# Retention attention with float32 scores in every unit, one bank pair a unit, and a prologue in a fixed order

## The chip, the cores and the metric

One core of one Trainium2 chip. The metric is device time in microseconds (us) of one execution; the kernel before takes 932.51 us in the median of three runs (931.04 to 933.9).

## What is computed

Three stages in a row, all float32: a linear attention with a decay for each head, and two feed-forward layers with unusual activations.

```python
# q, k, v: (4, 8, 768, 64); gamma per head
state = gamma * state + k_t (outer) v_t;  y_t = scale * q_t @ state      # for t in 768
x = y as 3072 tokens x 512
h = x @ w_in (512 x 2048);   g = h if h >= 1, 0 if h <= -1, else (h + 1)**2 / 4
x2 = g @ w_out (2048 x 512)
h = x2 @ w2_in (512 x 1024); solu = h * softmax(h); out = layernorm(solu) * g_ln @ w2_out
```

The weights of both layers arrive as float64.

## The kernel before

**Attention in units.** The recurrence is done in chunks of 128 tokens, six chunks a batch and four batches: 24 units. A unit (`attention`, L131) has *scores* (keys times queries, decayed by the table `dmat`, giving `sm`) and *products*: `pv` takes the state of the units before (L206, with `qn`, the decayed queries) and `sm` times values (L210); `sp` (L216) is the unit's own contribution to the state. `split` (L88) cuts `pv` into a rounded part `xh` and a remainder `xl`. Heads go in pairs; a head has 64 rows, so o = 0 and o = 1 are the two halves of the array. Units 0 to 7 multiply scores in float32 (L163). Units 8 to 23 load every half twice, make a rounded key with its remainder stacked below it and a rounded query with its remainder beside it, and multiply those (L188, 256 columns), add two result halves (L191, L192) and apply the table (L193).

**Tokens in blocks, features in slots.** Four units make a block of 512 tokens, six blocks in all. A slot is one block against one piece of 128 features: `moe_h` (L299), 12 products into `hp` (L306), then the activation (L312 to L314) and its split into `gh`, `gl`; two slots later `moe_out` (L320), 12 products into four accumulators `acc` (L334). All 12 have 512 columns in the rounded float32 format. The slots run in segments: block 0 with features 0 to 5, block 1 with 0 to 11, block 0 with 6 to 15, block 1 with 12 to 15, then blocks 2 to 5 whole. Blocks 0 and 1 therefore write a part of their sum to DRAM (`x2p`) and load it again at the end of their second segment (L346), through the ring of three `cs` buffers that the activation uses too.

**Weights.** `load_w` (L96) brings a float64 piece of 512 KB, `conv_w` (L101) makes a rounded part and a remainder from it on VectorE and ScalarE, five VectorE instructions a piece, two pieces a feature. This happens in the slots of the first four segments.

**What sets the order.** The Tile framework orders the instructions by its own timing model. The queue SP issues every DMA in program order, and each engine runs its own queue in order. Scores and products of a unit take buffers of one bank each (`ps_acc` in block 0, then `ps_a`).

**The last stage** (L402 on) goes by tiles of 128 tokens: `h2p`, softmax and norm statistics, transposes `tp`, products `op`. The change touches in it only how `h2` gets two of its banks.

Of the kernel before, what the change touches and what calls it, by code (L numbers as in the profile page):

```python
# [9 lines left out]
F32 = mybir.dt.float32  # L10
# [12 lines left out]
C = 128  # L23
# [12 lines left out]
NF32 = 2 * CPB  # L36
GATE = 2 * CPB
STEP0 = 7
W0 = -4
WARM = 40  # L40
PER = 4
# [8 lines left out]
def kernel(  # L50
# [16 lines left out]
    ve, sc, gp, pe = nc.vector, nc.scalar, nc.gpsimd, nc.tensor  # L67
# [7 lines left out]
    ps_a = ctx.enter_context(tc.tile_pool(name="ps_a", bufs=2, space=bass.MemoryType.PSUM))  # L75
# [18 lines left out]
    state = {}  # L94

    def load_w(src, pool=wp):  # L96
        raw = pool.tile([128, 512, 2], U32, tag="w", name="w_raw")
        state["last_w"] = nc.sync.dma_start(raw.rearrange("p a t -> p (a t)"), src.bitcast(U32))
        return raw

    def conv_w(raw, scale=None):  # L101
# [10 lines left out]
        ve.scalar_tensor_tensor(mu, hw, 0x80000000, mu, op0=ALU.bitwise_and, op1=ALU.bitwise_xor)  # L112
        ve.tensor_tensor(out=mi, in0=mi, in1=p.bitcast(I32), op=ALU.add)  # L113
        w = wp.tile([128, 2, 512], F32R, tag="w", name="w")
        hi, lo = w[:, 0, :], w[:, 1, :]
        if scale is None:
            sc.activation(hi, m, AF.Copy)
            ve.tensor_tensor(out=lo, in0=m, in1=fl(hi), op=ALU.subtract)
# [3 lines left out]
        return hi, lo  # L122


# [6 lines left out]
    def attention(u, env):  # L131
# [4 lines left out]
        ppool, ptag = (ps_acc, "acc") if blk == 0 else (ps_a, "pa")  # L136
        exact = u < NF32
        kv = (wp if exact else attp).tile([128, 2, H, D], F32, tag="w" if exact else "kv", name="kv",
                                          bufs=None if exact else 1)
        qn = None  # L140
        with (ExitStack() if u < GATE else tc.issue_after(state["last_w"].ins)):
            if exact:
                qk = wp.tile([128, 2, NPAIR, C], F32, tag="w", name="qk")
                nc.sync.dma_start(qk, qk_t[b, c])
            else:
                qks = []
                for o in range(2):
                    qk = attp.tile([128, 2, NPAIR, C], F32, tag="qk", name="qk", bufs=2)
                    for dup in range(2):
                        nc.sync.dma_start(qk[64 * dup:64 * dup + 64], qk_t[b, c, 64 * o:64 * o + 64])  # L150
                    qks.append(qk)
                if not first:
                    qn = attp.tile([128, NPAIR, C], F32, tag="qn", name="qn", bufs=1)
                    nc.sync.dma_start(qn, qk_t[b, c, :, 0])
            nc.sync.dma_start(kv, kv_t[b, c])
        yield
        if exact:
            yield
            qp = [ppool.tile([128, NPAIR, C], F32, tag=ptag, name=f"qp{o}") for o in range(2)]
            for p in range(NPAIR):  # L160
                for o in range(2):
                    r = slice(64 * o, 64 * o + 64)
                    pe.matmul(qp[o][:, p, :], qk[r, 1, p, :], qk[r, 0, p, :], start=True, stop=True)  # L163
            if not first:
                qn = attp.tile([128, NPAIR, C], F32, tag="qn", name="qn", bufs=1)
                ve.tensor_tensor(out=qn, in0=qk[:, 0], in1=qdec, op=ALU.mult)
        elif not first:
            gp.tensor_tensor(out=qn, in0=qn, in1=qdec, op=ALU.mult)
        if not last:
            gp.tensor_tensor(out=kv[:, 0], in0=kv[:, 0], in1=vdec.to_broadcast([128, H, D]), op=ALU.mult)  # L170
        sm = []
        for o in range(2):
            t = attp.tile([128, NPAIR, C], F32, tag="sm", name="sm", bufs=2)
            if exact:
                ve.tensor_tensor(out=t, in0=qp[o], in1=dmat[:, o], op=ALU.mult)
            else:
                raw = qks[o]
                kh = cv.tile([128, NPAIR, C], F32R, tag="wm", name="kh", bufs=3)
# [5 lines left out]
                yield  # L184
                for g in range(2):
                    qpo = ppool.tile([128, 2, 2, C], F32, tag=ptag, name=f"qp{g}")
                    for p in range(2):
                        pe.matmul(qpo[:, p].rearrange("a b c -> a (b c)"), kh[:, 2 * g + p, :],  # L188
                                  qs[:, 2 * g + p].rearrange("a b c -> a (b c)"), start=True, stop=True)
# [5 lines left out]
            if not exact and o == 0:  # L195
                yield
# [22 lines left out]
        if last:  # L219
            return  # L220
# [346 lines left out]
```

## Time and profile before

| | |
|---|---|
| median of 3 runs | 932.51 us |
| profiled execution | 931.13 us, span 929.3 us |
| TensorE (PE) busy | 909.6 us, 98% |
| VectorE (DVE) | 700.1 us, 75% |
| ScalarE (ACT) | 395.8 us, 43% |
| GpSimd (POOL) | 48.3 us, 5% |
| granted TensorE clock, mean | 0.995 |
| DMA | 87.16 MB, mean 94 GB/s |

Busy time is a union of intervals whose ends are modelled, so 98% does not say that PE runs at its rate. To see where it does, count instructions: a stretch of the span holds so many products, each product has a shortest spacing in steady work, and what is left of the stretch was lost. The span has four parts: the prologue to the first `hp` product, the slots of blocks 0 and 1 with the weight conversion, the slots of blocks 2 to 5 with the remaining attention, and from about 644 us on the last stage.

### The profile page before, as it was taken

What the parts mean: (1) busy time and instruction counts of PE and PEld (TensorE: products, weight loads), DVE (VectorE), ACT (ScalarE), POOL (GpSimd) and SP (SyncE); (2) the same over time, 40 slices, a digit from 0 to 9 for tenths busy, and PEclk for the clock granted to TensorE, in tenths of its full rate; (3) what the DMA queues carried; (4) which work ended last, traced back from release to release, by engine and by line L of the source; (5) the groups of instructions that cost most, each with busy time, mean ns of one, the idle gap of its engine ahead of it and who ended that gap; (6) DMA issues with size and microseconds to landing.
All of it is one profiled execution on the core that took longest, in us unless ns stands there. A gap on an engine that the chain in (4) does not pass through costs nothing.

```text
span 929.3 us, 12929 instructions
## 1 busy us (share of the span) xinstructions
PE 909.6 (98%) x4808; PEld 754.5 (81%) x4808; DVE 700.1 (75%) x1542; ACT 395.8 (43%) x757; POOL 48.3 (5%) x42
## 2 busy tenths in 40 slices
PE   8898999999889999999999999999999999999998
PEld 7686888888768888888888888888888888888886
DVE  5999999846675666676576549953988888888884
ACT  3656766533444444444444327632333333333322
POOL 3200101000101110011100000000000000000000
PEclk9999999999999999999999999999999999999999
DMA  9930752205553323332234104121101010100000
GB/s 342 417 137 1 238 159 75 84 1 153 153 170 94 100 81 98 96 93 78 69 103 152 53 1 160 45 94 46 45 35 68 24 68 24 68 24 23 24 23 35
DMA packets 29839, 87.16 MB, mean 94 GB/s; under 512 B 4176, under 2 KB 4304, under 8 KB 29008
## 3 DMA queue, kind: packets, MB, share of 16 engines
q1 hardware_dynamic: 29776, 86.34, 28.5%
q8 instruction: 38, 0.62, 0.3%
q14 instruction: 25, 0.20, 0.1%
HBM read 71.64 MB, written 14.68 MB: 93 GB/s over the span
## 4 chain that ended last, share of the span: by engine, by line
PE 91%; DVE 5%; DMA 2%; issue 1%; ACT 0%; SPq 0%; POOL 0%; ACTq 0%; DVEq 0%; POOLq 0%
PE acc L334 27%; PE hp L306 27%; PE h2p L433 14%; PE op L485 14%; PE tp L474 2%; PE pv L210 2%; PE pv L206 2%; PE qp L188 1%; DMA qk<-in_qk_t_dram 1%; PE sp L216 1%; PE qp L163 1%; DVE wm L112 1%; DVE wm L113 1%; DMA xs<-x2p 1%; DMA vdec<-in_vdec_dram 0%
## 5 line engine op out<-in xcount | busy, mean ns | idle before, releaser
L306 PE MATMUL hp<-xh,w 128*128 128x512 f32 x768 | 200.1, 395 | 7.2 <-DVE cs L314 2.9
L334 PE MATMUL acc<-gh,w 128*128 128x512 f32 x768 | 198.4, 391 | 1.6 <-DVE xs L347 1.6
L306 PEld LDWEIGHTS hp<-xh,w 128*128 128x128 f32 x768 | 141.9, 189 | 38.5 <-DVE cs L314 3.7
L334 PEld LDWEIGHTS acc<-gh,w 128*128 128x128 f32 x768 | 143.1, 188 | 32.3 <-DVE xs L347 2.3
L313 ACT ACTIVATE cs<-cs,half 128x512 f32<-128x512 f32 x96 | 69.3, 723 | 138.9 <-DVE cs L312 138.5
L334 PE MATMUL acc<-gl,w 128*128 128x512 f32 x384 | 110.7, 391 | 0.0
L306 PE MATMUL hp<-xl,w 128*128 128x512 f32 x384 | 105.7, 392 | 0.1
L433 PE MATMUL h2p<-w,x2h 128*128 128x512 f32 x384 | 97.0, 395 | 0.0
L312 DVE TENSOR_SCALAR cs<-hp 128x512 f32<-128x512 f32 x96 | 65.8, 688 | 39.1 <-PE hp L306 36.0
L90 DVE TENSOR_TENSOR gl<-cs,gh 128x512 fp32r<-128x512 f32 x96 | 68.4, 713 | 33.0 <-ACT gh L89 32.5
L314 DVE TENSOR_TENSOR cs<-hp,cs 128x512 f32<-128x512 f32 x96 | 66.1, 690 | 35.3 <-ACT cs L313 35.1
L485 PE MATMUL op<-w,lh 128*128 128x512 f32 x384 | 91.3, 390 | 0.2 <-ACT lh L89 0.2
L89 ACT ACTIVATE gh<-cs 128x512 fp32r<-128x512 f32 x96 | 60.4, 629 | 58.4 <-DVE cs L314 58.2
L306 PEld LDWEIGHTS hp<-xl,w 128*128 128x128 f32 x384 | 72.0, 189 | 15.6 <-DVE xl L90 0.5
L485 PEld LDWEIGHTS op<-w,lh 128*128 128x128 f32 x384 | 71.9, 188 | 15.3 <-ACT lh L89 0.5
L334 PEld LDWEIGHTS acc<-gl,w 128*128 128x128 f32 x384 | 71.6, 188 | 15.1
L433 PEld LDWEIGHTS h2p<-w,x2h 128*128 128x128 f32 x384 | 70.5, 188 | 13.7
L443 ACT ACTIVATE e<-h2p,st 128x512 f32<-128x512 f32 x48 | 32.6, 685 | 50.1 <-DVE st L460 38.3
L182 DVE TENSOR_TENSOR kh<-qk,kh 64x512 fp32r<-64x512 f32 x32 | 25.4, 793 | 36.8 <-ACT kh L180 36.5
L433 PE MATMUL h2p<-w,x2l 128*128 128x512 f32 x192 | 51.6, 390 | 0.0
L89 ACT ACTIVATE x2h<-x2r 128x512 fp32r<-128x512 f32 x24 | 15.1, 631 | 76.8 <-PE h2p L433 59.5
L485 PE MATMUL op<-w,ll 128*128 128x512 f32 x192 | 47.7, 390 | 0.0
(76 smaller groups left out, 1169.4 us busy)
## 6 DMA issues: line engine op xcount, KB each, us to landing
qk<-in_qk_t_dram SPq DMA_DIRECT2D x64, 256.0 KB, 3.9
kv<-in_kv_t_dram SPq DMA_DIRECT2D x24, 512.0 KB, 4.6
w_raw<-in_w_in_dram SPq DMA_DIRECT2D x24, 512.0 KB, 8.4
w_raw<-in_w_out_dram SPq DMA_DIRECT2D x24, 512.0 KB, 5.8
x2d<-xs SPq DMA_DIRECT2D x24, 256.0 KB, 3.2
x2r<-x2d SPq DMA_DIRECT2D x6, 1024.0 KB, 4.8
out_dram<-o SPq DMA_DIRECT2D x24, 256.0 KB, 2.0
qk<-in_qk_t_dram SPq DMA_DIRECT2D x8, 512.0 KB, 8.7
```

The costliest lines, as they stand in the source:

```text
L89: sc.activation(hi, src, AF.Copy)
L90: ve.tensor_tensor(out=lo, in0=src, in1=fl(hi), op=ALU.subtract)
L182: ve.tensor_tensor(out=kh[64:128], in0=raw[64:128, 1], in1=fl(kh[64:128]), op=ALU.subtract)
L206: pe.matmul(pv[:, p, :], st[:, p, :], qn[:, p, :], start=(p == 0), stop=False, skip_group_check=True)
L306: pe.matmul(hp, l[:, k * 128:(k + 1) * 128], r[:, k, :], start=(n == 0), stop=(n == 3 * KD - 1))
L312: ve.tensor_scalar(cs, hp, -1.0, 1.0, op0=ALU.max, op1=ALU.min)
L313: sc.activation(cs, cs, AF.Square, bias=half, scale=0.5)
L314: ve.tensor_tensor(out=cs, in0=hp, in1=cs, op=ALU.max)
L334: pe.matmul(acc[d][:, :BLK], l[:, d * 128:(d + 1) * 128], r, start=(first and m == 1), stop=(last and m == 3))
L433: pe.matmul(hps[n], l[:, k, :], w2i[k, n][part], start=(m == 0), stop=(m == 3 * KD - 1))
L443: sc.activation(e[:, n, :], hps[n], AF.Exp, bias=st[:, 2:3], accum_out=st[:, 3 + n:4 + n])
L485: pe.matmul(op, l[:, f, :], w2o[f][part], start=(n == 0), stop=(n == 3 * NF2 - 1))
```

## The change

What it does, part by part:

- **Scores.** All 24 units take the float32 path. The rounded copies, the doubled loads, the two additions and the separate load of `qn` go. A unit has one pair of banks (`bank`): its scores, then its products `pv` in the first and `sp` in the second. Units of block 0 other than unit 2 take the pair from `ps_acc`, all others take the single buffer of `ps_a`, which is now one buffer of two banks. From unit 8 on `sm` is one VectorE instruction of 1024 elements.
- **Tables.** `dmat` and `qdec` are no longer loaded as 128 rows. One row of 1024 numbers (`xrow`) is loaded by the ScalarE queue and spread over the partitions by products with a row of ones; VectorE multiplies the result by `vdec` or `gdec`.
- **Prologue.** Block 0 and the conversion of the first weight piece are written out in a fixed order, scores a unit ahead of the products. `issue` chains the instructions of each engine so that the scheduler keeps that order. Loads of the first weights stand between the loads of block 0. The warming products go from 40 to 18.
- **Later units.** Steps are given out as load, scores and products, six or seven, two and no slots ahead; two buffers each for keys/queries and keys/values.
- **Activation.** `(relu((h+1)/2))**2`, clipped at 1 and joined with h: two ScalarE instructions and one of VectorE, where there were two of VectorE and one of ScalarE.
- **Reload.** `xs` comes back through the ScalarE queue; the stores stay on SP.

```diff
-    ps_a = ctx.enter_context(tc.tile_pool(name="ps_a", bufs=2, space=bass.MemoryType.PSUM))
+    ps_a = ctx.enter_context(tc.tile_pool(name="ps_a", bufs=1, space=bass.MemoryType.PSUM))
...
+    @contextmanager
+    def issue(fixed, engines=None):
+        done = {i.name for i in nc.cur_bb.bb.instructions}
+        yield
+        for i in nc.cur_bb.bb.instructions:
+            if i.name in done or (engines and i.engine not in engines):
+                continue
+            if i.engine in tail:
+                tc.add_manual_dep(i, tail[i.engine].name, mybir.DependencyInfo(
+                    mybir.DependencyClass.NoSync, mybir.DependencyReason.DATA), reason="order of issue")
+            if fixed:
+                tail[i.engine] = i
...
+        if blk == 0 and u != 2:
+            pa = None
+            bank = [ps_acc.tile([128, 512], F32, tag="acc", name=f"pa{o}") for o in range(2)]
+        else:
+            pa = ps_a.tile([128, 2, 512], F32, tag="pa", name="pa")
+            bank = [pa[:, o] for o in range(2)]
+        qp = [t.rearrange("a (p c) -> a p c", p=NPAIR) for t in bank]
+        for p in range(NPAIR):
+            for o in range(2):
+                r = slice(64 * o, 64 * o + 64)
+                pe.matmul(qp[o][:, p, :], qk[r, 1, p, :], qk[r, 0, p, :], start=True, stop=True)
...
-                qs = attp.tile([128, NPAIR, 2, C], F32R, tag="qs", name="qs", bufs=1)
-                sc.activation(kh, raw[:, 1], AF.Copy)
-                sc.activation(qs[:, :, 0, :], raw[:, 0], AF.Copy)
-                ve.tensor_tensor(out=kh[64:128], in0=raw[64:128, 1], in1=fl(kh[64:128]), op=ALU.subtract)
-                ve.tensor_tensor(out=qs[:, :, 1, :], in0=raw[:, 0], in1=fl(qs[:, :, 0, :]), op=ALU.subtract)
-                        pe.matmul(qpo[:, p].rearrange("a b c -> a (b c)"), kh[:, 2 * g + p, :],
-                                  qs[:, 2 * g + p].rearrange("a b c -> a (b c)"), start=True, stop=True)
...
+    def make_dmat():
+        t = ps_a.tile([128, 2, 512], F32, tag="pa", name="tab")
+        for o in range(2):
+            pe.matmul(t[:, o], ones, xrow[:, o].rearrange("a p c -> a (p c)"), start=True, stop=True)
+            ve.tensor_tensor(out=dmat[:, o], in0=t[:, o].rearrange("a (p c) -> a p c", p=NPAIR),
+                             in1=vdec[:, o::2].to_broadcast([128, NPAIR, C]), op=ALU.mult)
+            gp.affine_select(out=dmat[:, o], in_=dmat[:, o], pattern=[[0, NPAIR], [1, C]], compare_op=ALU.is_ge,
+                             fill=0.0, base=0, channel_multiplier=-1)
...
-        ve.tensor_scalar(cs, hp, -1.0, 1.0, op0=ALU.max, op1=ALU.min)
-        sc.activation(cs, cs, AF.Square, bias=half, scale=0.5)
-        ve.tensor_tensor(out=cs, in0=hp, in1=cs, op=ALU.max)
+        sc.activation(cs, hp, AF.Relu, bias=half, scale=0.5)
+        sc.activation(cs, cs, AF.Square)
+        ve.scalar_tensor_tensor(cs, cs, 1.0, hp, op0=ALU.min, op1=ALU.max)
...
-                    nc.sync.dma_start(xs, x2p[blk][:, d, :])
+                    sc.dma_start(xs, x2p[blk][:, d, :])
...
+    with issue(True):
+        sc.dma_start(xrow, xtab_d.rearrange("(a o d) p c -> d a o p c", a=1, o=2)[0])
+        sc.dma_start(gdec, gdec_d)
+        sy.dma_start(vdec, vdec_d)
+        ve.memset(ones, 1.0)
+        att(0, 2)
+        att(1, 2)
+        att(2, 2)
+        att(3, 1)
+        load_wi(0)
+        att(3, 1)
+        load_wi(1)
+        load_wo(0)
+        load_wo(1)
+        make_dmat()
...
+        cv0 = conv_steps(wraw[0][0], wi, 0)
```

**The products of units 1 and 2 on PE.** Before, the scores of unit 2 stand in two groups, one for each half of the array (`qp_295`, `qp_296`), between the products of unit 1:

```order
L206 MATMUL pv<-qn,state 128x128 x4
L216 MATMUL sp<-kv 64x64 x8
L210 MATMUL pv<-sm,kv 64x128
L163 MATMUL qp_295<-qk 128x128 x4
L210 MATMUL pv<-sm,kv 64x128 x7
L163 MATMUL qp_296<-qk 128x128 x4
```

In the change the spread of `qdec`, the products of unit 0, the scores of unit 2 (both halves in turn, one buffer `pa`) and the products of unit 1 follow in this order:

```order
L256 MATMUL tab<-xrow,ones 64x512 x2
L209 MATMUL pa_159<-sm,kv 64x128 x8
L214 MATMUL pa_160<-kv 64x64 x8
L182 MATMUL pa<-qk 128x128 x8
L205 MATMUL pa_169<-qn,state 128x128 x4
L209 MATMUL pa_169<-sm,kv 64x128 x8
L214 MATMUL pa_170<-kv 64x64 x8
```

The two halves of a unit's scores, which stood apart, now alternate, and they stand ahead of the products of the unit before.

**The end of block 1's last segment on PE**, where units 11 and 12 meet the first slots of block 2. Before (`qp_2210` and `qp_2215` are the last scores of unit 11, `qp_2371`, `qp_2376` and `qp_2422` the first of unit 12):

```order
L188 MATMUL qp_2210<-qs,kh 128x256 x2
L188 MATMUL qp_2215<-qs,kh 128x256 x2
L206 MATMUL pv<-qn,state 128x128 x4
L210 MATMUL pv<-sm,kv 64x128
L188 MATMUL qp_2371<-qs,kh 128x256 x2
L210 MATMUL pv<-sm,kv 64x128 x7
L306 MATMUL hp<-xh,w 128x512 x5
L188 MATMUL qp_2376<-qs,kh 128x256 x2
L306 MATMUL hp<-xh,w 128x512 x11
L306 MATMUL hp<-xl,w 128x512 x8
L188 MATMUL qp_2422<-qs,kh 128x256 x2
```

In the change, behind the last `acc` of block 1:

```order
L182 MATMUL pa<-qk 128x128 x8
L205 MATMUL pa<-qn,state 128x128 x4
L209 MATMUL pa<-sm,kv 64x128 x8
L324 MATMUL hp<-xh,w 128x512 x16
L182 MATMUL pa<-qk 128x128 x8
L324 MATMUL hp<-xl,w 128x512 x8
L209 MATMUL pa<-sm,kv 64x128 x8
L214 MATMUL pa<-kv 64x64 x8
```

Unit 11's scores and products stand in one piece, and unit 12's scores come once, between the first two slots of block 2; no group waits for a second load of the same keys.

## Rows read from the trace of the kernel before

**Rows 1.** Busy time of each engine in three stretches (us, engine busy and count, clock).

```profile
28.00:98.00 70.00, 64.72 (x392) 50.88 (x392) 68.43 (x130) 42.69 (x76) 3.87 (x2) 0.98 0.41 163
98.00:229.00 131.00, 131.00 (x642) 108.45 (x642) 108.03 (x186) 71.46 (x128) 8.70 (x6) 1.00 0.39 115
229.00:283.00 54.00, 48.66 (x310) 39.08 (x309) 37.55 (x65) 23.64 (x50) 6.67 (x5) 1.00 0.59 169
```

**Rows 2.** Chain that ended last, in order of time: start, us, what; steady work.

```profile
278.15 0.89 PE pv L206 x8
279.04 1.02 PE pv L210 x16
280.06 0.47 PE sp L216 x16
...
286.01 0.47 PE qp L188 x4
...
503.30 2.72 PE acc L334 x12
```

**Rows 3.** PE's groups by shape between 27.78 and 109.1 us.

```profile
L306 PE MATMUL hp<-xh,w 128*128 128x512 f32 x89 | 25.3, 421 | 4.4 <-ACT w L117 2.1 <-DVE cs L314 0.8 <-DVE w L118 0.8
L334 PE MATMUL acc<-gh,w 128*128 128x512 f32 x72 | 18.9, 393 | 0.0
L306 PE MATMUL hp<-xl,w 128*128 128x512 f32 x44 | 12.6, 401 | 0.1
L334 PE MATMUL acc<-gl,w 128*128 128x512 f32 x36 | 10.8, 399 | 0.0
```

**Rows 4.** The same groups between 229 and 283 us.

```profile
L334 PE MATMUL acc<-gh,w 128*128 128x512 f32 x52 | 15.3, 401 | 1.6 <-DVE xs L347 1.6
L306 PE MATMUL hp<-xh,w 128*128 128x512 f32 x48 | 12.6, 402 | 2.8 <-DVE cs L314 2.1 <-ACT xh L89 0.8
L334 PE MATMUL acc<-gl,w 128*128 128x512 f32 x26 | 9.2, 396 | 0.0
L306 PE MATMUL hp<-xl,w 128*128 128x512 f32 x24 | 6.5, 391 | 0.0
...
L188 PE MATMUL qp<-qs,kh 128*128 128x256 f32 x24 | 4.6, 292 | 0.0
```

**Rows 5.** The chain between 215 and 300 us: two of its transfers.

```profile
244.06 4.15 DMA qk<-in_qk_t_dram
...
263.32 4.72 DMA xs<-x2p
```

**Rows 6.** The chain of the prologue.

```profile
1.72 4.53 DMA vdec<-in_vdec_dram
...
9.23 0.70 DVE sm L175
...
12.94 1.09 PE qp L163 x16
...
15.95 1.08 PE qp L163 x8
...
19.14 1.09 PE pv L206 x8
```

**Rows 7.** PE in order of time: start, us, what, idle before; first slot, and a late weight.

```profile
27.78 0.50 PE L306 MATMUL hp<-xh,w 128*128 128x512 f32 x1 [0.69 <-ACT xh L89]
...
76.11 4.35 PE L306 MATMUL hp<-xh,w 128*128 128x512 f32 x12 [2.12 <-ACT w L117]
```

**Rows 8.** VectorE in order of time; starts show its pace.

```profile
46.29 0.68 DVE L175 TENSOR_TENSOR sm<-qp,dmat 128x512 f32<-128x512 f32 x1
46.89 0.42 DVE L108 TENSOR_SCALAR wm<-wm 128x512 f32<-128x512 f32 x1
47.22 0.68 DVE L112 SCALAR_TENSOR_TENSOR wm<-w_raw,wm 128x512 uint32<-128x512 uint32 x1
```

**Rows 9.** The page on DMA: GB/s in 40 slices of 23.2 us, and a small load.

```profile
GB/s 342 417 137 1 238 159 75 84 1 153 153 170 94 100 81 98 96 93 78 69 103 152 53 1 160 45 94 46 45 35 68 24 68 24 68 24 23 24 23 35
...
ident<-in_ident_dram SPq DMA_DIRECT2D x1, 64.0 KB, 1.7
```

More of the change, by code (lines that the diff above doesn't have):

```diff
@@ L135, in attention @@
         attp = env["attp"]
[L136 to L155, printed above, removed]
@@ L156, in attention @@
-        yield
[L157 to L168, printed above, removed]
+        early = u < NWP
@@ new lines, in attention @@
+        yield
+        sm = tile_of([128, 2, NPAIR, C], "sm")
+        if early:
+            for o in range(2):
+                ve.tensor_tensor(out=sm[:, o], in0=qp[o], in1=dmat[:, o], op=ALU.mult)
+        else:
+            ve.tensor_tensor(out=sm, in0=pa.rearrange("a o (p c) -> a o p c", p=NPAIR), in1=dmat, op=ALU.mult)
+        yield
+        if not first:
+            qn = attp.tile([128, NPAIR, C], F32, tag="qn", name="qn", bufs=1)
+            ve.tensor_tensor(out=qn, in0=qk[:, 0], in1=qdec, op=ALU.mult)
@@ L217, in attention @@
                               start=True, stop=True)
-        split(pv, xh[:, :, tk], xl[:, :, tk])
-        if last:
-            return
-        if not first:
-            for p in range(NPAIR):
-                sc.activation(st[:, p, :], st[:, p, :], AF.Copy, scale=gdec[:, p, :])
-        for o in range(2):
-            r = slice(64 * o, 64 * o + 64)
-            if first:
-                ve.tensor_copy(st[r, :, r], sp[r])
-            else:
-                ve.tensor_tensor(out=st[r, :, r], in0=sp[r], in1=st[r, :, r], op=ALU.add)
+        yield
+        if not last:
+            if not first:
+                for p in range(NPAIR):
+                    sc.activation(st[:, p, :], st[:, p, :], AF.Copy, scale=gdec[:, p, :])
+            for o in range(2):
+                r = slice(64 * o, 64 * o + 64)
+                if first:
+                    ve.tensor_copy(st[r, :, r], sp[r])
+                else:
+                    ve.tensor_tensor(out=st[r, :, r], in0=sp[r], in1=st[r, :, r], op=ALU.add)
+        yield
+        split(pv, xh[:, :, tk], xl[:, :, tk])
     w2i, w2o = {}, {}
@@ L356 @@
             pe.matmul(wps[:, :128], wz, wz, start=(n == 0), stop=(n == WARM - 1))
[L357 to L361 removed]
+    with issue(True):
[13 more added lines that the diff above has]
+        make_dmat()
+        att(0, 1)
+        att(1, 1)
+        att(0, 1)
+        make_qdec()
+        att(0, 1)
+        att(1, 1)
+        att(0, 1)
+        att(1, 1)
+        cv0 = conv_steps(wraw[0][0], wi, 0)
+        for u in range(CPB):
+            if u + 2 < CPB:
+                att(u + 2, 1)
+            att(u, 1)
+            if u == 3:
+                next(cv0)
+            att(u, 1)
+            if u >= 2:
+                next(cv0, None)
+            if u + 1 < CPB:
+                att(u + 1, 1)
+            if u + 2 < CPB:
+                att(u + 2, 2)
+    with issue(False):
+        for s in range(min(min(sched), -LD - 1), 0):
+            att_slot(s)
+            weights_slot(s)
     w2 = [(w2_in[k, n], (k, n), w2i, None) for k in range(KD) for n in range(2)] + \
```

153 lines of the change are left out of this document (79 added, 74 removed).

## The prediction, made before the change was run

> **What bounds the kernel now.** I read the stretches first, then PE's spacing in steady work, then what the chain says where PE falls behind it. In the stretch from 98 to 229 us PE is never idle, and VectorE is at 108 of 131 us [rows 1]. In steady work twelve products of 512 columns take 2.72 us, 0.227 us each [rows 2]; a slot is 24 of them, 5.44 us. So from 98 us on PE sets the time, except where it stops, and it stops in two places.
>
> The first is the start. The first `hp` product begins at 27.78 us [rows 7]. From there to 109.1 us PE does 89+72+44+36 = 241 products of 512 columns [rows 3], which need 54.6 us, and the units 4 to 7. A unit's products take 0.89+1.02+0.47 = 2.38 us [rows 2] and its scores 1.09 us when the two halves alternate [rows 6], so four units need 13.9 us. Of 81.3 us some 13 are lost. VectorE is busy 68.4 of 70 us there [rows 1], and PE's longest stop, 2.12 us, is for a weight piece [rows 7]: conversion and attention share VectorE, and VectorE is the bound.
>
> The second is the stretch from 229 to 283 us: 150 products of 512 columns [rows 4] are 34.0 us, three units or a little more (24 score products are three units [rows 4]) 10 to 13 us, of 54 us. PE is idle 5.3 us by its records [rows 1], and by the count 7 to 10 us are lost. The chain there runs through loads of 4.15 us for keys and of 4.72 us for `xs` [rows 5]: buffers come free late, the loads are issued late, and PE waits.
>
> The profiled execution took 931.13 us, 1.8 us more than its span of 929.3, and 1.4 us less than the median of 932.51. I make the sum against it and add nothing for the median.
>
> **The change part by part.**
>
> *Scores in float32, units 8 to 23.* Now eight products of 256 columns; four take 0.47 us, a unit 0.94 us [rows 2]. Then 1.09 us when the halves alternate [rows 6]: +0.15 us in 16 units, **+2.4 us** on PE, which is the bound there. Where one half stands alone it takes 1.08 us [rows 6], so a unit 2.17 us; that bound is +1.23 x 16 = +19.7 us. The order has the halves in turn in every unit, so I take +2.4. By the Trainium skill (FP8 and Floating Point Precision, TensorE Precision Notes) true float32 takes four passes through the array; as an estimate by that page a score product of 128 columns would cost what 512 columns do. Eight of them would be 1.8 us in a row, and the sum would gain 14 us in place of 2.4; the row of 1.09 us shows two halves running beside each other, which the page's sentence leaves out.
>
> *What goes from VectorE, ScalarE and SP in those units* (copies, subtractions, additions, doubled loads) costs nothing and gives nothing by itself: PE covers it from 98 us on [rows 1]. If PE waited there, the longer `sm` of 1024 elements, about two steps of 0.60 us [rows 8], would show.
>
> *Activation.* VectorE loses one 0.60 us step a slot, ScalarE gains one. ScalarE is busy 42.7 of 70 us in the tight stretch [rows 1]; eight more instructions of its usual length leave it below 50. The chain from `hp` to `gl` keeps five links.
>
> *Tables and prologue.* `sm` of unit 0 starts at 9.23 us, after the 4.53 us of a small load that stood behind a megabyte [rows 6]. Now `xrow` is first on its own queue; a 64 KB load takes 1.7 us [rows 9], so it is there near 3 us. Its products have no row; they lie between 0.45 us (two passes of 0.227) and 1.1 us (four times a lone 128-column product) each; I take 0.9, nearer to the float32 row. Then the table is multiplied and masked near 6 us, three us earlier. But PE's order has unit 1's scores and `qdec`'s products ahead of unit 0's products. They wait for the fourth load: 512 KB at the 417 GB/s of the second slice [rows 9] are 1.26 us, so after some 4.5 us for the first, unit 1's keys land near 8, and unit 0's products start near 10, as they do now. What is won is the pace. Now units 1 and 2 are about 5 us apart, because halves of scores at 1.08 us stand inside the loop of state, products and state [rows 6]. With the scores ahead, the loop is 0.89 (state) plus ScalarE's scaling and VectorE's addition, 3.6 us. Three units later, with the first weight piece converted between them on VectorE and ScalarE, the first `hp` starts near **26 us** instead of 27.78. Not before 21 (16 us for the ten loads up to unit 3's values, then one unit), not after 28.5 (the clock halved while PE waits for loads).
>
> From there the order gives VectorE 22 steps of 0.33 us, 57 of 0.60 and four state additions of 0.43 up to unit 7's scores: 43.2 us [rows 8]. It will stop where `xl` waits for products of units 5 to 7, some 5 us by my placing, and PE waits for it in places: the second weight piece 2.2 us, the first `gh` and `gl` 1.4, later weights and activations 2, the single bank pair, which holds unit 5's and unit 6's scores until the remainder before is taken, 1 each, and 1.5 around unit 7. That is 9 us lost in place of 13 plus what halves alone cost units 5 to 7. Block 1's segment then starts near 80 us, as now, but with six `acc` groups done rather than four. At the state that PE has at 109.1 us now it arrives near 103: **-6 us**. Bounds: -12 if VectorE never stops, +1 if PE loses its clock in the longer waits.
>
> *Later units and the reload.* Keys of unit 11 wait for unit 9's buffer, and by the order 19 us of PE work stand between that and unit 11's scores, so the 4.15 us are covered. Left are the stops between unit 11's scores, products and first `hp`, about 1.1 us. `xs` now waits on ScalarE: the first of block 1's four is issued only behind the relu of the second slot of block 2, and the fourth waits for a store that stands on SP behind unit 14's loads. I place the last addition 24 us after block 1's last `acc`; by the order PE has four `hp` groups, unit 12's scores and products, unit 13's scores and most of two `acc` groups to do by then, 23 us. So some 3.5 of the 7 to 10 us remain: **-5.5 us**, bounds -9 and 0.
>
> *The last stage* runs at PE's pace; `h2` taking two banks as one buffer waits for VectorE's later half, which is long done. Nothing.
>
> Sum: 929.3 + 2.4 - 6 - 5.5 = 920.2 us, and 1.8 around it: **922 us**.
>
> **The rivals.**
>
> *The prologue brings little.* VectorE's 43 us of work stay, and PE starts no earlier in effect because the fixed order makes it wait for loads; -1.5 in place of -6 gives 926.5 us. For it: VectorE at 98% [rows 1]. Against: a step less a slot and no halves alone.
>
> *The reload stays as dear.* ScalarE, blocked behind the load of `xs`, holds up the activations; the middle gives nothing, 927.5 us. For it: the same ring of three buffers, and the order of SP. Both together: 932 us, no change to be measured.
>
> *The halves do not overlap* in the new places, one bank pair and units squeezed between 512-column products: +19.7 in place of +2.4 gives 939 us, slower. It decides from 0.9 us a unit, where it eats both gains. Against it: 1.09 us was measured for alternating halves; in the order every unit has them so. A page of the Trainium skill (TensorEngine Tiling (Array Packing), Key Properties) says that a change of tiling mode drains the engine, which speaks for it; the 0.47 us of eight 64-column pairs between full products [rows 2] shows no such price.
>
> **How the numbers follow.** My forecast 0.58; the prologue brings little 0.14; the reload stays 0.11; both 0.09; halves apart 0.05; another slower case, such as a wait on ScalarE's queue in every block, 0.03. A measurement of this kernel can tell about 0.3%, 2.8 us, from no change. The first three are faster, 0.83; both is the same, 0.09; the rest slower, 0.08. The range reaches from 913 (prologue -12, middle -8) to 929 and takes in the first three.
>
> **What would show it.** Right: a score group of 1.09 us in units 8 to 23; first `hp` near 26 us; about 103 us for the state of 109.1; no load of keys in the chain between 225 and 285 us, and under 4 us lost there. Wrong: scores of 2 us; a first `hp` after 28; PE waiting for `xs` or for an activation behind it for over 3 us; a clock at half for more than two of the short stretches before 100 us.

## The result, and the profile after

The changed kernel takes 941.79 us (median of 4 runs, 939.39 to 942.59), the kernel before 931.77 us in the same comparison: 1.0100 times as long, 95% interval 1.0074 to 1.0127. The forecast was 922 us, in a range of 913 to 929. It was wrong in size and sign. The profiled execution took 941.62 us, with a span of 939.9 us.

The page's lines on the engines and the traffic, for the changed kernel:

```profile
PE 912.5 (97%) x4922; PEld 751.6 (80%) x4922; DVE 574.1 (61%) x1318; ACT 396.7 (42%) x725; POOL 28.4 (3%) x27
...
DMA packets 24543, 74.29 MB, mean 79 GB/s; under 512 B 3106, under 2 KB 3234, under 8 KB 23716
```

VectorE and the DMA queues have less to do, as the change says, and the time is longer: this is a matter of when, not of how much. The three stretches of [rows 1], now for the changed kernel:

```profile
28.00:98.00 70.00, 55.64 (x359) 44.01 (x355) 58.64 (x109) 42.25 (x78) 2.23 (x2) 0.91 0.37 138
98.00:229.00 131.00, 128.77 (x643) 106.34 (x641) 82.74 (x144) 77.41 (x134) 8.61 (x3) 0.99 0.24 86
229.00:283.00 54.00, 50.36 (x363) 40.97 (x358) 25.45 (x38) 16.34 (x30) 3.16 (x3) 1.00 0.51 152
```

In the first one PE lost 9 us of busy time, VectorE fell from 68.43 to 58.64 us, and the mean granted clock from 0.98 to 0.91. PE's groups between 27.78 and 109.1 us, as in [rows 3]:

```profile
L324 PE MATMUL hp<-xh,w 128*128 128x512 f32 x77 | 25.7, 480 | 13.0 <-ACT xh L104 6.9 <-ACT w L134 3.1 <-DVE cs L332 2.2
L352 PE MATMUL acc<-gh,w 128*128 128x512 f32 x52 | 14.1, 399 | 1.8 <-ACT gh L104 1.7
L324 PE MATMUL hp<-xl,w 128*128 128x512 f32 x36 | 10.0, 406 | 0.0
L352 PE MATMUL acc<-gl,w 128*128 128x512 f32 x24 | 6.9, 390 | 0.0
```

These are 77+52+36+24 = 189 products of 512 columns where there were 241, beside the same four units: 52 x 0.227 = **11.8 us behind** at 109.1 us, more than the 10.6 us by which the span has grown. The same shows when the products of 512 columns that fill the slots (2304 in all) are counted in the order of their starts (us):

| start of the | before | change | tie2q (below) |
|---|---|---|---|
| 121st | 80.3 | 71.6 | 81.8 |
| 241st | 108.9 | 122.0 | 109.0 |
| 1100th | 344.3 | 353.5 | 344.6 |
| 2304th | 643.7 | 654.2 | 645.3 |

The change is 9 us ahead at the 121st product, with the products of three of the four units still to do, and 13 behind at the 241st (11.8 when the scores of unit 8, which only the change has done by then, are taken off). All of the loss is decided there. Where it comes from shows in VectorE's and PE's rows, ten microseconds at a time (columns as in [rows 1]):

```profile
60.00:70.00 10.00, 9.88 (x84) 8.11 (x83) 9.92 (x20) 6.78 (x14) 0.00 (x0) 1.00 0.33 115
70.00:80.00 10.00, 8.27 (x63) 6.64 (x62) 5.57 (x10) 3.06 (x5) 0.00 (x0) 1.00 0.12 44
80.00:90.00 10.00, 7.96 (x99) 6.41 (x97) 4.70 (x9) 3.00 (x8) 0.00 (x0) 1.00 0.00 0
90.00:100.00 10.00, 6.41 (x16) 5.06 (x17) 9.89 (x21) 7.64 (x14) 0.00 (x0) 0.66 0.01 2
```

VectorE, the bound of this stretch before, is idle for 9.7 of the 20 us from 70 to 90 us, and PE waits beside it. A part of the loss is the clock: the 16 products from 93.59 us on, behind a wait of 3.87 us, took 6.60 us, 0.41 each in place of 0.227, at a granted clock of 0.66 from 90 to 100 us. That is 3 us more. And in order of time, the scores of unit 4 (PE, L182), the `sm` that is made of them (DVE, L187), its products (PE, L205), and then the handover after unit 7 on ScalarE and PE:

```profile
35.66 1.16 PE L182 MATMUL pa<-qk 64*128 64x128 f32 x16
...
57.76 1.27 DVE L187 TENSOR_TENSOR sm<-pa,dmat 128x512 f32<-128x512 f32 x2
...
60.12 0.72 PE L205 MATMUL pa<-qn,state 128*128 128x128 f32 x5
...
91.77 0.63 ACT L134 ACTIVATE w<-wm 128x512 fp32r<-128x512 f32 x1
92.31 0.65 ACT L125 ACTIVATE wp<-w_raw 128x512 f32<-128x512 uint32 x1
92.94 0.60 ACT L104 ACTIVATE xh<-pa 128x512 fp32r<-128x512 f32 x1
...
93.59 0.79 PE L324 MATMUL hp<-xh,w 128*128 128x512 f32 x1 [3.87 <-ACT xh L104]
```

`sm` starts 22 us after the scores. The same two steps before the change are 4.4 us apart:

```profile
28.90 0.83 PE L163 MATMUL qp<-qk 64*128 64x128 f32 x10
...
33.27 1.28 DVE L175 TENSOR_TENSOR sm<-qp,dmat 128x512 f32<-128x512 f32 x2
```

So unit 4 holds the one bank pair for 25 us, units 5 to 7 bunch up behind it, and PE meanwhile does the products of the segment. PE's order, counted in finished groups of twelve ahead of each unit's products:

| products of | before: `hp`, `acc` groups ahead | after | tie2q (below) |
|---|---|---|---|
| unit 4 | 1.0, 0 | 4.3, 3.0 | 1.0, 0 |
| unit 5 | 2.0, 1.0 | 5.3, 5.0 | 2.0, 1.0 |
| unit 6 | 3.0, 2.0 | 6.0, 5.3 | 3.0, 2.0 |
| unit 7 | 4.3, 3.0 | 6.0, 6.0 | 4.0, 3.0 |

Unit 7 now comes when nothing of the segment is left to do in its waits, unit 6 when two thirds of an `acc` group are. From 78 to 94 us PE stops for `gh`, for `sm` and for `xh`, 7 us in all. The order on PE is not all of it, though: tie2 (below) has nearly the counts of tie2q, and its units' products come 13 to 16 us later than tie2q's.

### The profile page after: what moved, and what is told of

The parts are those of the page before. It is cut to its first block, busy times and chain, and to the rows that moved or that the text cites. A ratio compares the mean times of both kernels' runs of the same rounds, so it can differ in the third digit from the quotient of the medians.

```text
span 939.9 us, 12653 instructions
## 1 busy us (share of the span) xinstructions
PE 912.5 (97%) x4922; PEld 751.6 (80%) x4922; DVE 574.1 (61%) x1318; ACT 396.7 (42%) x725; POOL 28.4 (3%) x27
## 2 busy tenths in 40 slices
DMA packets 24543, 74.29 MB, mean 79 GB/s; under 512 B 3106, under 2 KB 3234, under 8 KB 23716
## 4 chain that ended last, share of the span: by engine, by line
PE 88%; DVE 5%; DMA 1%; ACT 1%; issue 1%; ACTq 0%; DVEq 0%; SPq 0%
PE acc L352 27%; PE hp L324 26%; PE h2p L495 14%; PE op L547 14%; PE tp L536 2%; PE pa L182 2%; PE pa L209 2%; PE pa L205 1%; DVE wm L127 1%; DVE wm L129 1%; PE pa L214 1%; DVE wm L123 1%; DMA x2d<-xs 1%; DVE w L136 1%; DVE cs L332 0%
## 5 line engine op out<-in xcount | busy, mean ns | idle before, releaser
L324 PE MATMUL hp<-xh,w 128*128 128x512 f32 x768 | 199.3, 400 | 13.7 <-ACT xh L104 7.6
L324 PEld LDWEIGHTS hp<-xh,w 128*128 128x128 f32 x768 | 146.3, 192 | 46.9 <-ACT xh L104 8.2
L332 DVE SCALAR_TENSOR_TENSOR cs<-cs,hp 128x512 f32<-128x512 f32 x96 | 65.7, 684 | 162.6 <-ACT cs L331 162.5
L330 ACT ACTIVATE cs<-hp,half 128x512 f32<-128x512 f32 x96 | 65.9, 686 | 192.4 <-PE hp L324 177.5
L105 DVE TENSOR_TENSOR gl<-cs,gh 128x512 fp32r<-128x512 f32 x96 | 66.1, 688 | 38.2 <-ACT gh L104 37.9
L495 PEld LDWEIGHTS h2p<-w,x2h 128*128 128x128 f32 x384 | 70.5, 188 | 13.7
L331 ACT ACTIVATE cs<-cs 128x512 f32<-128x512 f32 x96 | 60.5, 630 | 2.5
L502 DVE TENSOR_REDUCE st<-h2p 128x1 f32<-128x512 f32 x48 | 32.0, 687 | 18.4 <-PE h2p L495 18.3
```

What stands on the lines that cost most here:

```text
L105: ve.tensor_tensor(out=lo, in0=src, in1=fl(hi), op=ALU.subtract)
L324: pe.matmul(hp, l[:, k * 128:(k + 1) * 128], r[:, k, :], start=(n == 0), stop=(n == 3 * KD - 1))
L330: sc.activation(cs, hp, AF.Relu, bias=half, scale=0.5)
L331: sc.activation(cs, cs, AF.Square)
L332: ve.scalar_tensor_tensor(cs, cs, 1.0, hp, op0=ALU.min, op1=ALU.max)
L495: pe.matmul(hps[n], l[:, k, :], w2i[k, n][part], start=(m == 0), stop=(m == 3 * KD - 1))
```

## The experiments

All times are medians; ratios are to the kernel before on the same chip, with 95% intervals. Against the changed kernel's 1.0100 a ratio of 0.001 is 0.9 us.

**One cause at a time.** First the clock, ScalarE's queue and the first handover. More warming products:

```diff
-WARM = 18
+WARM = 40
```

> The changed kernel with 40 warming products in place of 18, as before. Clock theory (the prologue runs at half clock because 18 products end too soon): the granted clock is full from about 6 us instead of 17.4, the two units' scores take 2.2 us instead of 3.7, unit 0's products start near 12 us instead of 13.7, the first hp product near 29.5 instead of 31.2, and the time falls by 1.5 us (1 to 3), to about 940. The table products start later, near 5.4 us, so dmat comes hardly earlier. Queue theory (ScalarE's order decides): the first hp comes earlier, but the wait for the second weight piece and the one for unit 7's xh near 90 us take it back; 0 to -1 us.

Measured: 941.34 us, 1.0101 (1.0077 to 1.0125), no gain. The products that spread the tables do get faster, in the groups of the first 20 us, of the change and of this run:

```profile
L247 PE MATMUL tab<-xrow,ones 1*128 1x512 f32 x4 | 4.1, 1129 | 0.8 <-DVE dmat L248 0.8
```

```profile
L247 PE MATMUL tab<-xrow,ones 1*128 1x512 f32 x4 | 2.2, 640 | 0.8 <-DVE dmat L248 0.8
```

but they start later, behind 22 more warming products, and the scores of the first two units took 3.7 us as before, not 2.2, at a granted clock of 0.56 to 0.59 from 8 to 12 us. Unit 0's products took 1.09 us where the change's profile has 1.98, and the first `hp` started at 29.4 us in place of 31.2, as the clock theory had it. But the early start stands in profiles with 18 warming products too (29.2 us in xh7, 29.4 in sm1) and is missing in one with 40 (31.0 in sm1w; all three below): it differs between executions, and more warming products don't secure it. It is worth a few microseconds to a single execution at most (the three with the early start took 939.44, 937.87 and 935.72 us, 1.3 to 4.9 under their medians), and even these are over the kernel before. (The granted clock of the change's first ten microseconds reads 1.00 although its products there stand at nearly twice the spacing of this run's; I go by the spacing.)

Then the state update and the split of unit 7, ordered ahead of the conversions of the later pieces:

```diff
-        with (issue(False) if s < SA else ExitStack()):
+        with (issue(False) if s < 2 * SA else ExitStack()):
             weights_slot(s)
...
         with (issue(False) if s < SA else ExitStack()):
             g = moe_h(blk, f)
+        with (issue(s == SA - 1, (sc.engine, ve.engine) if s == SA - 1 else None) if s < SA else ExitStack()):
             att_slot(s)
```

> The changed kernel, only with unit 7's state update and its split (xh, xl) ordered ahead of the weight conversions of the later pieces, on ScalarE and on VectorE. Queue theory: the 3.9 us that PE waits near 90 us shrinks to about 1, the half clock of 92.5 to 99.4 us does not come, the wait of 2.2 us for an activation behind it goes too; time -6 us (-4 to -9), about 936. Bank pair theory (units 4 to 7 are slow because one bank pair holds them one after another, and VectorE has nothing to do in between): the wait only moves, at most -1 us, about 941. Clock theory (only the prologue's warming counts): 0.

Measured: 939.20 us, 1.0080 (1.0060 to 1.0101): -2.6 us by the medians and -1.9 by the ratios, under half of what was expected, and the intervals overlap. PE's waits between 80 and 110 us tell why; in the change, and then in this run:

```profile
PE hp L324 <- ACT xh L104: 3.9, 1, 3.9
PE hp L324 <- DVE cs L332: 2.2, 1, 2.2
```

```profile
PE hp L324 <- DVE cs L332: 3.4, 1, 3.4
PE hp L324 <- ACT xh L104: 1.7, 1, 1.7
```

The wait for `xh` shrank, the one for the activation behind it grew: VectorE was still idle before 90 us (busy for 4.89 and 4.38 of 10 us from 70 to 90) and late after it. Unit 3's split ahead of the first piece's last steps (its `split` moved ahead of the state update for `u == 3`), alone and with the two edits above:

> The changed kernel, only with unit 3's split ahead of the first weight piece's last steps and of its state update. Queue theory: the first hp starts near 29.8 us instead of 31.2, and up to 1.4 us of that stays, -1 us in the time, about 941. Load theory (the weight loads come late because eight units' sm, the ones and the row share the 33 buffers): the second weight piece is what hp waits for near 40 us, so 0.

Measured: 944.92 us, 1.0138 (1.0115 to 1.0162). The first `hp` came 2.5 us earlier, at 28.70 us, and the time rose by 3 by the medians. 1.7 of the 2.5 us are not the edit's: unit 3's scores already start that much earlier in this execution.

> All three edits in one. Queue and clock theories together: first hp near 28 us, the waits near 90 us gone, -9 us (-6 to -12), about 933, no slower than before the change. Bank pair and load theories: at most -3 us, about 939.

Measured: 943.48 us, 1.0120 (1.0098 to 1.0143), no faster than the change. Three plausible repairs don't add up. The next runs change what stands ahead of the places where PE waits.

**The buffers.** In the change `sm` of eight units, `ones` and the row, ten tiles, were added to the pool of 33 buffers that holds the weights and the loads of units 0 to 7. The first run takes `sm` of units 4 to 7 out again.

```diff
-            if early:
+            if early and (name != "sm" or u < CPB):
                 return wp.tile(shape, F32, tag="w", name=name)
```

> The changed kernel, only with sm of units 4 to 7 in the one buffer that sm of the later units has, and no longer in the 33 buffers of the weights. Buffer theory (converted pieces find no free buffer among the 33, so the conversions stand behind units 6 and 7 in VectorE's queue and VectorE is idle for some 9.7 of the 20 us from 70 to 90 us): VectorE is busy over 8 of every 10 us there, the conversions lie between the units, PE's waits from 90 to 110 us (3.9 and 2.2 us) go; time -6 us (-4 to -10), about 935.5. Queue theory (only what stands before unit 7's xh on ScalarE counts): that order hardly changes, at most -3 us. Bank pair theory: units 6 and 7 take as long as before, VectorE fills its idle time but PE's waits stay; 0 to -2 us.

Measured: 940.60 us, 1.0086 (1.0062 to 1.0109), not the 935.5 expected. `sm` of unit 4 now runs at 37.57 us, 20 us earlier, and VectorE is over 9 of 10 us busy from 70 to 100. The time hardly moves. With units 4 and 5's queries, keys and values moved too (`if early and u not in (4, 5) and (name != "sm" or u < CPB)`):

> As the run with sm of units 4 to 7 in its own buffer, and with the keys, queries, keys and values of units 4 and 5 also in the buffers that units 8 and on use, four more of the 33 free. Buffer theory: another -1 to -2 us, about 934, and weight loads that follow each other more closely from 30 to 50 us. Others: the same as the run before, within 1 us.

Measured: 938.75 us, 1.0078 (1.0062 to 1.0095). VectorE is filled there, in this run:

```profile
70.00:80.00 10.00, 10.00 (x70) 8.10 (x68) 9.89 (x20) 8.39 (x15) 0.00 (x0) 1.00 0.16 54
80.00:90.00 10.00, 7.31 (x70) 5.49 (x68) 9.96 (x21) 7.42 (x15) 0.00 (x0) 1.00 0.00 0
```

but with conversions: 15 pieces are finished when block 1 starts, where the kernel before has 12, and unit 7's `xl` comes at 92.6 us (70.7 before). An idle engine was a sign, not the cause. The granted clock from 90 to 100 us is 1.00 here (0.66 in the change) and the time only 3 us less, so the clock is at most a part of it.

The `sm` edit with 40 warming products:

> As the first run of these, with 40 warming products. Buffer theory with VectorE as the bound up to 100 us: an earlier first hp is taken back by the conversions, within 1 us of the first run. Clock theory: 1.5 us faster than the first run.

Measured: 939.42 us, 1.0089 (1.0069 to 1.0109): the same as without the 22 products. And the changed kernel with no fixed order (no dependence is added in `issue`):

> The changed kernel with no fixed order in the prologue: all else is the change's, and the scheduler places every instruction. If the fixed order costs (loads waited for in turn): the first hp comes before 31 us and the time falls by 1 to 3 us. If the order is what gives the 3.7 us pace of the units: the first hp comes 1 to 4 us later, and the time rises by as much or stays, since the buffers decide the rest. Buffer theory: VectorE stays idle from 70 to 90 us.

Measured: 943.99 us, 1.0118 (1.0099 to 1.0136). In its profile, of an execution of 949.16 us, the first `hp` comes at 35.8 us, 4.6 later, and VectorE is idle as before (busy for 3.96 and 5.04 of 10 us from 70 to 90). The fixed order is worth about 2 us by the medians, within the intervals; it isn't the culprit.

**Place and buffers together.** Units 4 to 7 are tied to the slots, in the order of the program on three engines, two slots earlier in it, with scores one slot ahead:

```diff
-        x = SA - CPB + k if blk == 1 else base[blk] - NF + 4 * k + 2
-        for n, steps in ((x - (STEP0 if blk == 1 else 6), 2), (x - 2, 3), (x, 3)):
+        x = SA - CPB + k - 2 if blk == 1 else base[blk] - NF + 4 * k + 2
+        for n, steps in ((x - (STEP0 if blk == 1 else 6), 2), (x - (1 if blk == 1 else 2), 3), (x, 3)):
...
-        with (issue(False) if s < SA else ExitStack()):
+        with (issue(True, (pe.engine, ve.engine, sc.engine)) if s < SA else ExitStack()):
             g = moe_h(blk, f)
             att_slot(s)
```

tie2 is this edit; tie2s adds the edit of sm1, tie2q that of sm1qk; tie1q is tie2q one slot later.

> The changed kernel, with units 4 to 7 tied to slots 1 to 4 of block 0 on PE, VectorE and ScalarE (scores one slot, not two, ahead of their products; the buffers as in the change). Position theory (what costs the time is that units 5 to 7 slide behind the segment's last products, so that PE has nothing left to do in their waits): unit 7's xl ends before 75 us instead of 95.6, the sixth slot's first hp comes near 80 instead of 93.6, PE's loss up to 120 us falls from 40 to 30 us or less, time -8 us (-5 to -11), about 934. Buffer theory (sm in the weights' buffers decides): the tie alone cannot help, since sm of unit 4 still waits for a buffer; PE then stops behind it, 0 or slower, up to +5. Clock theory: 0.

> As the run before, and with sm of units 4 to 7 in the one buffer of its own. Position theory alone: the same as the run before within 1 us. Position and buffers together: sm of unit 4 comes within 5 us of its scores, 3 us faster than the run before, about 931.

> As the run before, and with queries, keys and values of units 4 and 5 out of the weights' buffers too. Position and buffers: 0 to -1.5 us against the run before, about 930. If VectorE's own work (conversions wanted in time for the slots) is the bound, no difference.

> As the run before, but with units 4 to 7 tied to slots 2 to 5. Position theory: units one slot later leave PE one group less to fill in with, 1 to 2 us slower than the run before; if only the order among the units counts and not the place, the same.

Measured: tie2 942.04 us, 1.0104 (1.0085 to 1.0123); tie2s 942.62, 1.0110 (1.0094 to 1.0126); **tie2q 932.77, 1.0002 (0.9989 to 1.0014)**; tie1q 939.19, 1.0077 (1.0060 to 1.0095). The four corners, in us:

| | buffers as in the change | `sm` of 4 to 7, and units 4 and 5's loads, out of them |
|---|---|---|
| units placed by the scheduler | 941.79 | 938.75 |
| units tied to slots 1 to 4 | 942.04 | 932.77 |

Each repair alone gives 0 to 3 us, both give 9 (by the ratios 1.0100, 1.0078, 1.0104 and 1.0002). `sm` alone is not enough, against what I expected of tie2s: it runs there 3.4 us after unit 4's scores (at 40.6 and 37.2 us), and the time is tie2's. Only with the loads of units 4 and 5 out of the pool too, which I expected to bring 1.5 us at most and which brought 10, do unit 4's scores stand ahead of the first `hp`, at 26.2 us, and its products start at 33.8 us in place of 43.9. No run takes the loads out without `sm`, so whether it is these tiles or the number of buffers freed, eight in place of four, stays open. The parts of the tie (order, slots, scores one slot ahead) were not tried one by one; tie1q moves the slots alone.

What SP's queue waits for from 28 to 75 us shows what the full pool does; before the change, in the change, in tie2 and in tie2q:

```profile
SPq L98 <- DVE wm L112: 6.5, 3, 4.4
```

```profile
SPq L112 <- DVE wm L127: 21.4, 6, 9.0
```

```profile
SPq L112 <- DVE wm L127: 22.6, 5, 8.1
```

```profile
SPq L112 <- DVE wm L127: 14.7, 2, 10.6
```

In the change and in tie2 the loads of raw pieces wait six and five times until a conversion gives up a buffer: none goes out from 30.7 to 40.0 us, and in tie2 VectorE is idle for 8 of the 20 us from 60 to 80. In tie2q the loads go out back to back until 40.3 us, as before the change (41.6). And VectorE's `sm` and finished pieces from 30 to 60 us, in the kernel before, the change and tie2q:

```profile
L118 DVE TENSOR_TENSOR w<-wm,w 128x512 fp32r<-128x512 f32 x6 | 4.1, 686 | 0.0
L175 DVE TENSOR_TENSOR sm<-qp,dmat 128x512 f32<-128x512 f32 x6 | 4.0, 685 | 0.1
```

```profile
L136 DVE TENSOR_TENSOR w<-wm,w 128x512 fp32r<-128x512 f32 x8 | 5.4, 675 | 0.0
...
L187 DVE TENSOR_TENSOR sm<-pa,dmat 128x512 f32<-128x512 f32 x2 | 1.3, 671 | 0.0
```

```profile
L136 DVE TENSOR_TENSOR w<-wm,w 128x512 fp32r<-128x512 f32 x8 | 5.7, 712 | 0.0
...
L187 DVE TENSOR_TENSOR sm<-pa,dmat 128x512 f32<-128x512 f32 x6 | 3.9, 686 | 0.0
```

Before, three units pass in these 30 us; in the change one, at the very end; in tie2q three again. In tie2q PE has done by 109.1 us:

```profile
L324 PE MATMUL hp<-xh,w 128*128 128x512 f32 x89 | 23.1, 399 | 2.3 <-ACT xh L104 2.0 <-DVE w L136 0.3
L352 PE MATMUL acc<-gh,w 128*128 128x512 f32 x72 | 21.5, 438 | 6.6 <-ACT w L134 3.2 <-ACT gh L104 3.0 <-DVE w L136 0.4
L324 PE MATMUL hp<-xl,w 128*128 128x512 f32 x44 | 11.8, 390 | 0.0
L352 PE MATMUL acc<-gl,w 128*128 128x512 f32 x36 | 10.5, 401 | 0.0
```

241 products again, the very count of [rows 3]. The 11.8 us are accounted for. tie1q, one slot later, costs 6.4 us of them, more than the 1 to 2 expected of the place.

**Why only level, and what the middle rests on.** Four more, on tie2q and on the kernel before.

> The version with units 4 to 7 tied to slots 1 to 4 and with their sm, and units 4 and 5's queries, keys and values, out of the weights' buffers (932.8 us), and unit 3's split ahead of the first piece's last steps and of its state update. Position and buffers settled, so a start that is earlier should now be kept: first hp 28.0 instead of 29.4 us, time -1 us (0 to -2), about 931.7. If VectorE is the bound from 30 to 60 us: 0.

> The same version (932.8 us), with units 4 to 7 one slot earlier still, in slots 0 to 3. Position theory: earlier units leave more of the segment's products for later; 0 to -2 us. If VectorE is the bound: the units' steps now stand ahead of conversions that the first slots need, +1 to +3 us. This tells whether the place is a matter of the earlier the better.

Measured: tie2qu 933.67 us, 1.0016 (1.0005 to 1.0027); tie3q 935.63 us, 1.0034 (1.0022 to 1.0047). In tie2qu's profile the first `hp` came at 30.3 us, no earlier than in tie2q (29.4): the scores ahead of it stood 1.8 us later in this execution. So whether an earlier start is kept stays open. Earlier units don't help: of the three places tried, slots 1 to 4 are the best.

The reload on SP's queue in tie2q, and on ScalarE's in the kernel before:

```diff
-                    sc.dma_start(xs, x2p[blk][:, d, :])
+                    sy.dma_start(xs, x2p[blk][:, d, :])
```

> The same version (932.8 us), with the reload of xs on SP's queue, as before the change. If the queue is what shortens the stretch from 220 to 285 us: the losses there, 8.4 us, rise by 1.5 to 4 us, about 935.5. If it is the fewer loads and buffers of the float32 scores that do it: within 1 us.

> The kernel before the change, only with the reload of xs on ScalarE's queue. If the queue alone does it: the loss of 9 us from 240 to 280 us shrinks by 2 to 4, time -2 to -4 us, about 929.5. If the doubled loads of keys hold it up: 0 to -1 us.

Measured: tie2qsy 932.17 us, 0.9995 (0.9983 to 1.0007), the same as tie2q; b_reload (the opposite edit on the kernel before) 931.02 us, 0.9984 (0.9974 to 0.9994), 0.7 us by the medians and 1.5 by the ratio, less than expected of the queue. The reload's queue is not what shortens the middle.

A step of VectorE given to GpSimd, and then the conversions one slot later:

```diff
-            ve.tensor_tensor(out=qn, in0=qk[:, 0], in1=qdec, op=ALU.mult)
+            (gp if CPB <= u < NWP else ve).tensor_tensor(out=qn, in0=qk[:, 0], in1=qdec, op=ALU.mult)
```

> The version with units 4 to 7 tied to slots 1 to 4 and the buffers freed (932.8 us), and qn of units 4 to 7 multiplied on GpSimd. If VectorE is the bound from 30 to 70 us, its 4 x 0.60 = 2.4 us less give up to 2 us: about 931. If the order of the conversions among the units' steps decides, or GpSimd's own time on the way to the state products does: 0 to +2 us.

> The run before, with each weight piece converted one slot later in the program (three slots ahead of its use, not four), so that fewer pieces stand ahead of the units' steps and the activations: by the order 11 instead of 12 ahead of the fourth gl, 12 instead of 15 ahead of the sixth. If pieces converted too early are what holds up units and activations: another -1 to -2 us, about 929.5, faster than the kernel before. If pieces then come too late: PE waits for them, +1 to +3 us.

Measured: tie2qg 937.12 us, 1.0044 (1.0027 to 1.0061); tie2qgc3 (with `LD, CL = 7, 3`) 934.76 us, 1.0023 (1.0011 to 1.0036). Both slower than tie2q, the second by 2 us with intervals that just touch. VectorE's steps and GpSimd's between 28 and 80 us, in tie2q and then in tie2qg:

```profile
L129 DVE CUSTOM_DVE_ANT_0 wm<-wm,wp 128x1024 uint16<-128x1024 uint16 x13 | 8.9, 690 | 0.1
...
L105 DVE TENSOR_TENSOR gl<-cs,gh 128x512 fp32r<-128x512 f32 x4 | 2.8, 692 | 0.0
```

```profile
L129 DVE CUSTOM_DVE_ANT_0 wm<-wm,wp 128x1024 uint16<-128x1024 uint16 x12 | 9.4, 794 | 0.2
...
L105 DVE TENSOR_TENSOR gl<-cs,gh 128x512 fp32r<-128x512 f32 x4 | 3.6, 895 | 0.1
...
L193 POOL TENSOR_TENSOR qn<-qk,qdec 128x512 f32<-128x512 f32 x3 | 7.2, 2399 | 21.9 <-issue 19.2 <-PE pa L205 2.7
```

A step taken from VectorE is not a gain there: GpSimd needs 2.40 us for it on the mean, and 12 and 4 of VectorE's other steps are 0.10 and 0.20 us longer on the mean, 2 us in all of the 2.4 saved. These 2 us are three steps of 1.2, 1.5 and 1.5 us at the end of a `qn` and beside the two multiplies of `kv` that stand behind it on GpSimd. So the run does not settle whether VectorE's amount of work is what keeps tie2q from the forecast gain. Against tie2qg, converting later gave 2.4 us, in the direction expected: the order of the conversions counts. No version tried beats the kernel before by more than its interval but b_reload, and that by 0.16%.

## Why the prediction was wrong

*Scores in float32, +2.4 us: the row came, the price was too small.* In the chains of the kernel before and of the change a half unit's scores and a later unit's scores stand between products of 512 columns like this:

```profile
285.78 0.23 PE hp L306
286.01 0.47 PE qp L188 x4
286.48 2.52 PE hp L306 x11
```

```profile
288.59 1.13 PE hp L324 x5
289.72 1.09 PE pa L182 x16
290.81 1.82 PE hp L324 x7
```

The scores take the 1.09 us of [rows 6], in place of 0.94, and 16 x 0.15 = 2.4 us. But the twelve products around them take 2.95 us, 0.23 more than the 2.72 of [rows 2], and before only 2.75. So a unit costs 1.3 us in place of 1.0, and 16 units 5 us more. Over the seven units behind the 1100th product, where PE never waits, the change is 1.35 us longer, which would be 3 us for 16: the term is 3 to 5 us. The 0.47 us of [rows 2], from which the prediction read that a change of mode has no price, stands behind products of its own shape (128*64), and can't show one; that such a change is what the 0.23 us are was not tried. The estimate of 1.8 us by the four passes of the Trainium skill (FP8 and Floating Point Precision, TensorE Precision Notes) is not what eight products take where two halves run beside each other. The rival of halves that do not overlap forecast 939 us, near the result, and is refuted: the sum was near for another reason. (It would have eaten both gains from 0.72 us a unit, 11.5 us over 16, not from 0.9.)

*Later units and the reload, -5.5 us: about right in the change's profile, not in every run, and unsure in its reason.* From the 241st to the 1100th product the kernel before takes 235.4 us, the change 231.5, or 232.8 with unit 8's scores, which it has done earlier: -2.6 us with nine units' dearer scores inside, so some -4.5 to -5.5 for the term. tie2q's profile has 235.6 there, no gain, and tie2qsy's 232.5. The forecast laid the gain to the order of queues and to the loads. tie2qsy and b_reload take the reload's queue out of it; that it is the fewer loads (74.29 MB) and the shorter way to the scores is what remains, and was not tried by itself.

*Prologue and first slots, -6 us: this failed.* It came out at +12, by three steps of the text.

The pace was about right (unit 1's products to unit 2's 3.8 us, forecast 3.6) and the start was not. I priced two table products at 0.9 us each. Each is two instructions in the profile, four of 1.13 us with a stop of 0.8 us for VectorE's reading of the first half, 4.9 us in place of 1.8, and both units' scores stand behind them. Unit 0's products came at 13.7 us, not 10, and the first `hp` at 31.2, not 26 (29.2 to 32.2 in the runs that share this prologue, by how early its products come to full speed in the execution). Yet u3, with 28.7 us, gained no time, and warm40's execution with 29.4 us took 939.44: these 3 to 6 us of delay are not what the result is made of.

The sentence that costs is this: "Block 1's segment then starts near 80 us, as now, but with six `acc` groups done rather than four." I counted six groups done as work gained. They are the work with which PE covered the units' waits before; done early, they leave PE idle. Block 1 started at 93.6 us. This is the step that failed: I read the place of units 4 to 7 in PE's order and took the groups ahead of them for progress, without asking why the units came later.

And the reason why they came later was in the diff: ten more tiles, `sm` of eight units above all, in the weights' buffers. The forecast counted which buffer the keys of unit 11 wait for, and the single bank pair ("1 each"), but not what the 33 buffers hold in the first 90 us. Loads of raw pieces waited for conversions, `sm` of unit 4 stood behind conversions in VectorE's queue, and the bank pair was held until `sm`. The four corners show that the pool and the place together make the loss; this chain from one to the other is read from the rows above, and which of the eight tiles matter stays open. The bound of +1 us for this term took in only the clock. The rival that the prologue brings little was the right doubt, with a price too small: it kept the order as good as before.

*VectorE as the bound* was right in [rows 1] and misled me: a step less in each slot helps only if VectorE's order has something ready. After the change it had less work and was idle for 9.7 us where PE waited.

With place and buffers mended the level is reached but not passed: tie2q has 241 products at 109.1 us, the count of before, where the forecast had them at 103, and its profile doesn't show the gain of the middle either (the 1100th product starts at 344.6 us, before at 344.3), so nothing pays for the dearer scores behind it. What takes the 6 us between 28 and 80 us stays open. Its waits there (3.2 us for a piece's `w`, 3.0 for `gh`, 2.0 for `xh`) are all behind conversions on ScalarE or VectorE, and tie2qgc3 points to their order; no run shows it alone.

## What to carry to other kernels

When a change makes one kind of work come later than another, ask which of the two covered the other's waits: products without a wait are the reserve of an engine that sets the time, and doing them first is no gain. Count what a shared pool of buffers holds at each stage before giving it more tenants, since a full pool delays loads, and through in-order queues everything behind them. And two causes that act together look like no cause at all when they are mended one by one; try the pair before giving up either.

## What was not expected of the hardware

The three multiplies of 128x512 elements that tie2qg gives to GpSimd are recorded with 1.52, 2.94 and 2.73 us (0.68 on VectorE). Beside the two long ones eight VectorE steps keep their usual 0.68 us, and only the step at each end grows (1.16 us in place of 0.69, 0.90 in place of 0.42); beside the short one a VectorE step of usually 0.42 us takes 1.38, and beside GpSimd's multiply of `kv` one of the four `gl` steps takes 1.53 us (the others 0.69). So either engine's record can be the one that grows. The Trainium skill (SBUF — State Buffer, SBUF: two separate sides) says that the two share a port pair, which the one that starts first holds for its whole instruction while the other is blocked; longer steps on both sides agree with it, which engine held the pair is not seen. A group of float32 scores in alternating halves of 64 rows costs the products of 512 columns around it 0.23 us beyond its own 1.09. A product with one row of float32 weights and 512 columns is recorded as two instructions of about 1.1 us each in the change's profile and of 0.64 in warm40's: as dear as five to ten of the products that do the kernel's work.
